# A written order for four engines, carried from the first batch to the start of the third, in a fused attention and mixture kernel

## The chip, the cores and the metric

The program runs on one core of one Trainium2 chip. The metric is device time in microseconds (us), as the median of several executions; of the kernel before there are three, 648.04, 649.50 and 650.23 us. A further execution was profiled, and all rows shown here come from that one.

## The reference

Three stages follow each other, all in float32. B = 8 batches, H = 8 heads, 576 positions, head width 64, m = 32 landmarks:

```
q_lm, k_lm = means of q, k over 18 positions each
A, Bm, C = softmax(q k_lm'), softmax(q_lm k_lm'), softmax(q_lm k')
Z = Bm' / (norm_1 * norm_inf);  six times: Z = 2 Z - Z Bm Z
x = A Z C v                          # laid out as 4608 tokens x 512
h = silu(x w_gate) * (x w_val);  x = h w_out      # 1536 hidden units
logits = x phi                       # 32 slots, softmax over tokens and over slots
out = c @ (relu((d' x) w1) w2)       # 8 experts
```

The inputs w_gate, w_val and w_out arrive as 64-bit floats and are turned into 32-bit ones on the chip.

## The kernel before, in words

A prelude computes the attention factors of batch 0 (`first_attention`, lines 424 to 594) out to two small factors: the softmax A as tiles EH and EL (a high and a low part), and WB, a product of Z, C and v. Then come eight batches, numbered 0 to 7, each of 12 units of 128 hidden units (`unit`, line 1020). A unit has two halves of 288 tokens; each half has a gate product `pg` and a value product `pv`, six matmuls each on line 1017 (`mm3`), a Silu or Tanh on ScalarE into `u`, and a multiplication on VectorE into `hT` (line 1046). Beside the units run, spread over slots between them: `g` (line 820, WB times the gate weights, cast on ScalarE to GH and subtracted on VectorE to GL), `l` (line 866, logits from `hT`), a transposition of `hT` (line 871), the attention factors of the next batch (`attention` and `a_softmax`), and the slot softmax of the batch before (`softmoe`, matmuls `m_d` on line 985). In batch 0 the conversion of the weights runs too: for each 1 MB block of the gate and value weights (`load_w`) and each 512 KB block of w_out (`load_o`) a Prelu on ScalarE (line 235) takes the upper words, and two VectorE operations (lines 251 and 252) put in the lower bits; a converted block of w_out goes to `wo_dram` (line 306) and through three small products (`m_wt`, `m_p`, `m_ps`) into P_sb, which `l` reads.

What sets the order: each engine runs its instructions in program order. A scheduler chooses that order from its own costs, unless it is told. `ORDER` (line 55) tells it: for each engine a list of positions in the traced order of that engine's instructions, `a+n` being n positions from a on. `written_order` (line 123) chains the listed instructions. What is not listed comes behind the last listed one: on TensorE in traced order, on the other engines as the scheduler has it. All transfers are issued from the sync engine (SP) one after the other; one that has to wait for its buffer holds up those behind it.

Positions that the text names. TensorE before: 0 to 14 are the fifteen 1x1 warm matmuls of line 1092, 15 to 22 the first eight score matmuls, 23 to 30 the next eight; with three warm matmuls fewer, every later position is smaller by 3. ScalarE: 1 and 2 the first two Exp, 33 the Prelu on the first block of w_out, 192 the Exp on the first half of batch 2's A, 209, 212 and 215 Silu of batch 1, 210 and 211 the casts to EH of batch 2, 237 the Silu of the first half of batch 1's last unit. VectorE: 10 the scaling that the first Exp waits for, 12 the first transposition of A, 61 a shift for the first block of w_out. GpSimd: 21 and 22 the subtractions to EL of batch 2, 23 a small addition. SP: 27 and 28 the load of v for batch 1, whose 128 KB tail is 28 and whose 1 MB main part is 27; 31, 34 and 40 blocks 5, 6 and 7 of the gate and value weights; 58 to 61 the loads of k for batch 2.

The `l` of a unit needs both halves of its `hT`; it is issued in the slots of the next unit (line 1188), and TensorE waits there if VectorE is late with `hT`.

Of the kernel before, what the change touches and what calls it, by code (L numbers as in the profile page):

```python
# [53 lines left out]

ORDER = {
    'PE': '''
# [7 lines left out]
      839+4 855+6 895+6 919+8 907+6''',  # L64
    'DVE': '''
# [8 lines left out]
      242 237 241 239 238 244 255 247 256 252+2 246 248 245 257 267+2 254 261 258 270 249''',  # L74
    'Activation': '''
# [5 lines left out]
      162 167 166 168+2 171 170 173 172 174+2 177 180 179 181 176 178 183''',  # L81
    'Pool': '''
      0 3 2 4 1 16 6 5 8 7 9+3 15 12 14 13 18''',
    'SP': '''
      0+4 7 5+2 4 14 8+2 25 17 15 18 16 23 10 22 11 21 19 24 26 12+2 29 20 28 30+2 33 32 34 40 36 35 58 37
      39 38 41+3 46 45 59 44 48 47 27 60 50+2 61 49 52 64 53+2 57 56 65+7 55 72+2 62''',
}


# [1 line left out]
def nystrom_softmoe_kernel(  # L91
# [996 lines left out]
                next(gens[c], None)  # L1088

    m = psp.tile([128, 512], F32, tag="l", name="warm")  # L1090
    for _ in range(15):
        pe.matmul(m[0:1, 0:1], one, one, start=True, stop=True)
    first_attention(side)
    in_order("silu", warm, one, AF.Silu)
# [329 lines left out]
```

## Time and profile before

| | us |
|---|---|
| median of three executions | 649.50 (648.04 to 650.23) |
| the profiled execution | 649.76 |
| its span on the core | 648.0 |
| prelude, until the first unit | 38.0 |
| batch 0 | 76.0 |
| batch 1 | 68.0 |
| batch 2, batch 3 | 65.2, 65.1 |

The batches are bounded by the first `pg` matmul of each (at 38.0, 114.0, 182.0, 247.2 and 312.3 us of the trace). Times in the views are us from the start of the span; PE is TensorE, DVE VectorE, ACT ScalarE, POOL GpSimd, SP the sync engine. What lies around the span is 1.76 us.

### The profile page before, as it was taken

The numbers are of one execution on the slowest core, as the hardware profiler recorded it, in microseconds if no ns is written. First come the engines' busy times: TensorE is split into PE (matmuls) and PEld (weight loads), VectorE is DVE, ScalarE is ACT, GpSimd is POOL, SyncE is SP. The second block draws the span as 40 slices with busy tenths as digits, with TensorE's granted clock in tenths as the row PEclk, the third lists the DMA queues.
The fourth block names the chain that finished last, engine by engine and source line by source line (L and its number), as shares of the span: only waits on it lengthen the run. The fifth ranks groups of instructions, "written<-read, shape, count | busy, mean of one in ns | idle before, by whom it ended". The sixth has DMA issues, their size and how long they took to land. (4 is left out here: it accounts for less than half of the span.)

```text
span 648.0 us, 18273 instructions
## 1 busy us (share of the span) xinstructions
PE 617.2 (95%) x7589; PEld 465.6 (72%) x7589; DVE 465.4 (72%) x1139; ACT 301.2 (46%) x761; POOL 73.0 (11%) x81
## 2 busy tenths in 40 slices
PE   6999999999999999999999999999999999999991
PEld 2866778777878787878787878787878777743560
DVE  4999989797678687868786878687856656550441
ACT  1888975383266226622662256225623532411441
POOL 0320003030013001300130013001300000010100
PEclk9999999999999999999999999999999999999996
DMA  9999871424032023302420242022310696599999
GB/s 336 389 319 330 324 250 56 143 81 129 23 127 90 8 88 129 90 4 84 135 91 3 83 138 90 3 76 72 92 58 1 218 368 233 190 327 347 348 371 331
DMA packets 63298, 106.47 MB, mean 164 GB/s; under 512 B 4976, under 2 KB 33008, under 8 KB 61680
## 3 DMA queue, kind: packets, MB, share of 16 engines
q1 hardware_dynamic: 63216, 105.32, 48.4%
q8 instruction: 59, 0.97, 0.6%
q14 instruction: 23, 0.19, 0.1%
HBM read 91.24 MB, written 12.58 MB: 160 GB/s over the span
## 5 line engine op out<-in xcount | busy, mean ns | idle before, releaser
L375 ACT ACTIVATE u<-pg 128x288 f32<-128x288 f32 x169 | 69.6, 413 | 155.3 <-PE pg L1017 151.2
L1046 DVE TENSOR_TENSOR hT<-u,pv 128x288 f32<-128x288 f32 x169 | 75.4, 448 | 36.3 <-PE pv L1017 31.1
L1017 PE MATMUL pg<-EH,GH 128*128 128x288 f32 x384 | 93.1, 323 | 0.0
L851 DVE TENSOR_TENSOR GL<-g,GH 128x512 fp32r<-128x512 f32 (+1 forms) x114 | 65.1, 598 | 35.1 <-ACT GH L837 35.1
L1017 PE MATMUL pg<-EH,GL 128*128 128x288 f32 x384 | 84.5, 297 | 0.5
L1017 PE MATMUL pv<-EH,GH 128*128 128x288 f32 x384 | 83.8, 299 | 0.0
L1017 PE MATMUL pv<-EL,GH 128*128 128x288 f32 x384 | 82.1, 295 | 0.0
L1017 PE MATMUL pg<-EL,GH 128*128 128x288 f32 x384 | 82.1, 295 | 0.0
L1017 PE MATMUL pv<-EH,GL 128*128 128x288 f32 x384 | 81.9, 294 | 0.0
L837 ACT CAST GH<-g 128x512 fp32r<-128x512 f32 (+1 forms) x114 | 54.0, 521 | 50.8 <-PE g L820 50.7
L1017 PEld LDWEIGHTS pg<-EH,GH 128*128 128x128 f32 x384 | 59.4, 189 | 24.8 <-issue 20.2
L871 DVE STREAM_TRANSPOSE HB<-hT 128x576 f32<-128x576 f32 x96 | 74.1, 773 | 1.6
L1017 PEld LDWEIGHTS pg<-EH,GL 128*128 128x128 f32 x384 | 62.0, 188 | 2.6 <-DVE GL L851 2.6
L1017 PEld LDWEIGHTS pv<-EH,GH 128*128 128x128 f32 x384 | 61.2, 188 | 2.9 <-issue 1.9
L1017 PEld LDWEIGHTS pv<-EH,GL 128*128 128x128 f32 x384 | 61.6, 188 | 0.0
L1017 PEld LDWEIGHTS pg<-EL,GH 128*128 128x128 f32 x384 | 61.5, 188 | 0.0
L1017 PEld LDWEIGHTS pv<-EL,GH 128*128 128x128 f32 x384 | 61.5, 188 | 0.0
L820 PE MATMUL g<-w,WB 64*32 64x512 f32 (+1 forms) x912 | 55.3, 534 | 0.4 <-ACT HB L329 0.3
L866 PE MATMUL l<-hT,P_sb 128*32 128x160 f32 (+1 forms) x768 | 44.7, 298 | 2.6 <-DVE hT L1046 2.2
L866 PEld LDWEIGHTS l<-hT,P_sb 128*32 128x32 f32 x768 | 15.1, 108 | 40.2 <-DVE hT L1046 15.6
L985 PE MATMUL m_d<-HB,HB 32*32 32x384 f32 x864 | 35.3, 491 | 0.0
L985 PE MATMUL m_d<-HB,DN 32*32 32x384 f32 x288 | 35.1, 491 | 0.0
(255 smaller groups left out, 939.1 us busy)
## 6 DMA issues: line engine op xcount, KB each, us to landing
k<-in_kT_dram SPq DMA_DIRECT2D x52, 288.0 KB, 3.9
ffn<-in_w_dram SPq DMA_DIRECT2D x13, 1024.0 KB, 8.6
ffn<-in_w_dram SPq DMA_DIRECT2D x24, 512.0 KB, 8.9
HB<-in_w_cat_dram SPq DMA_DIRECT2D x8, 1024.0 KB, 8.5
v<-in_v_dram SPq DMA_DIRECT2D x8, 1024.0 KB, 6.8
q<-in_qT_dram SPq DMA_DIRECT2D x28, 288.0 KB, 3.0
HB<-in_w_out_dram SPq DMA_DIRECT2D x12, 512.0 KB, 6.4
wr<-in_w_cat_dram SPq DMA_DIRECT2D x4, 1024.0 KB, 7.5
```

The lines of the kernel that those rows point to most:

```text
L375: i = act.activation(*a, **kw)
L820: pe.matmul(gs[r][32 * hp:32 * hp + 32, 0:256 * n].rearrange("p (u f) -> p u f", u=n), WB[b % 2][64 * r:64 * r + 64, hp, :], w[64 * r:64 * ...
L837: act.copy(H_, g)
L851: dve.tensor_tensor(out=GL, in0=g, in1=GH, op=ALU.subtract)
L866: pe.matmul(L[32 * c:32 * c + 32, 0:32 * k], P_sb[:, j, :], main[:, 0:k, c, :], start=j == 0, stop=j == NJ - 1)
L871: dve.transpose(HB[b % 2][:, S * j:S * j + S].rearrange("p (t r) -> p t r", r=32), hT[:, 0:S].rearrange("p (t r) -> p t r", r=32))
L985: pe.matmul(ms[a][32 * g:32 * g + 32, 0:384].rearrange("p (j f) -> p j f", j=NJ), d_of(a, g, k), hb[32 * a:32 * a + 32, :, 4 * k + g, :], ...
L1017: pe.matmul(ps[:, 0:HALF], G_t[b, j, q, sel_][h], e[:, q, ts_], start=n == 0, stop=n == 5)
L1046: i = dve.tensor_tensor(out=o, in0=u, in1=pv[:, 0:HALF], op=ALU.mult)
```

## The change

The order lists are replaced. Those of TensorE, VectorE, ScalarE and GpSimd now reach further: on TensorE 1389 positions instead of 911, out to the score matmuls in the first unit of batch 2 (185 us of the trace of before, against 130 us); on VectorE 362 instead of 261, on ScalarE 243 instead of 183, on GpSimd 25 instead of 18. They also differ from the start on, within the stretch that was already written. The list of SP becomes shorter, 36 positions instead of 73; the transfers behind it come in the scheduler's order. Three of the fifteen warm matmuls are gone, and the other twelve stand behind the first eight scores. No operation is otherwise added or removed.

```diff
--- before.py
+++ after.py
@@ -54,36 +54,49 @@
 
 ORDER = {
     'PE': '''
-      0+47 55+4 47+8 59+14 76+4 73+3 80+11 92 94+4 93 118 91 119+5 98+20 144+2 124+20 146+4 154+2 150+4
-      156+14 182+12 170+12 194+45 243+10 259 253+6 260+18 239+4 300+6 284+8 296+4 278+6 292+4 312+19 337+8
-      349+4 306+6 331+6 345+4 365 353+6 366+12 402+4 378+8 359+6 386+6 406+6 418 392+6 423+6 419+4 412+6
-      435+8 447+4 429+6 451+6 463 398+4 457+6 443+4 464+18 492+4 482+6 496+8 510+45 556+6 555 568+8 504+6
-      562+6 488+4 584+2 580+4 592+7 586+6 599+6 576+4 605+12 621+6 633+6 627+6 617+4 639+5 658+8 644+2
-      670+4 646+12 688 674+8 689+4 682+6 693+2 666+4 695+12 711+4 721+7 715+6 740+6 728+4 768+6 732+2
-      750+12 734+6 707+4 774 746+4 762+6 775+12 791+22 787+4 831+8 819+6 813+6 825+6 843+12 861+6 871+24
-      839+4 855+6 895+6 919+8 907+6''',
+      12+8 0+12 20+24 52+4 44+8 56+15 73+4 71 77 72 78+6 89 84+4 90 115 91+4 116 95+20 141+2 88 117+24
+      143+4 151+2 147+4 153+14 179+8 167+6 187+10 173+6 197+39 240+4 250+11 244+6 261+8 236+4 269+6 281+8
+      297+6 293+4 275+6 309+19 303+6 350+6 334+8 328+6 346+4 356+6 289+4 362+5 342+4 367+8 383+6 375+8
+      399+4 395+4 389+6 415 403+6 416+4 432+8 420+6 409+6 444+4 426+6 448+6 460+5 440+4 454+6 465+4 473+6
+      469+4 495+6 489+6 479+6 507+45 485+4 553+6 552 501+6 565+8 581+2 559+6 583+6 577+4 589+6 600+2 595+5
+      573+4 602+12 630+6 618+6 636 614+4 637+4 624+6 655+8 641+8 667+4 649+6 671+8 663+4 679+25 718+6
+      712+6 737+6 708+4 765+6 724+7 704+4 747+12 743+4 731+6 759+6 772+6 771 778+10 804+6 788+16 816+6
+      810+6 828+8 822+6 840+24 892+6 868+24 836+4 904+6 916+8 898+6 864+4 928+6 910+6 940+6 934+6 924+4
+      966+6 956+10 946+6 990+8 978+6 972+6 952+4 984+6 1049+6 1002+40 1061+6 1043+6 1042 1055+6 998+4
+      1071+2 1145+6 1076 1073 1080 1077 1074 1078 1075 1084 1079 1081+2 1088 1085 1083 1087 1091 1095 1092
+      1096 1089 1093 1086 1090 1094 1097 1099+2 1104 1101 1098 1102+2 1107 1111 1115 1106 1110 1119 1105
+      1123 1114 1118 1109 1108 1122 1112 1126 1130 1134 1113 1116+2 1121 1120 1138 1125 1129 1133 1124
+      1127 1137 1142 1141 1128 1132 1136 1140 1131 1135 1139 1144 1143 1151+14 1171+8 1183+2 1067+4 1179+4
+      1165+6 1185+12 1241+8 1197+14 1215+2 1223+6 1217+6 1211+4 1229+6 1253+2 1235+6 1255+12 1249+4 1283+2
+      1267+16 1285+16 1307+6 1301+6 1313+6 1329+14 1319+6 1343+6 1355+6 1365+8 1349+6 1373+8 1325+4 1361+4
+      1381+8''',
     'DVE': '''
-      1 0 3 2 6 4 7 5 12 24 9 8 10 23 14+4 21 61 18 22 20 27 19 25 11 13 26 42 32 34 33 35+2 43 37 48 41
-      38 44 62 45+3 52 49 57 54 53 50 39 102 29 28 31 68 40 58 30 56 97 59+2 51 65 55 63+2 75 69 73 71 74
-      66 72 70 77 98 79 76 67 78 80+2 99 103 85+2 84 91 83 82 88 87 89+2 93+2 92 100+2 106 109 127 136 96
-      120 105 108 95 113 104 107 119 114 129 117 111 116 118 139 112 121 115 110 131 123 135 125 128 138
-      126 133+2 137 130 122 223 132 146 142 147 150 124 140 153 145 157 167 149 151 143+2 154 164 152 172
-      156 160+3 148 158 141 155 163 159 168 166 169+2 165 175 171 185 181 189 182+3 186 179 190+3 188
-      193+2 180 197 201 187 204 198 203 199 176 202 195 205+2 209 207 215 196 173 212+2 210 177 214 216
-      174 229 219 211 217 220 178 221 218 224 222 227+2 200 208 226 231 225 232+2 230 236 235 234 240 243
-      242 237 241 239 238 244 255 247 256 252+2 246 248 245 257 267+2 254 261 258 270 249''',
+      1 0 3 2 6 4 7 5 12 61 24 8+3 14+4 22+2 21 18 20 27 19 25 11 13 26 42+2 32+6 45 41 57 28 46 44 47 38
+      49 62 53 48 29 58 50 39 97 40 31 56 52 54 51 102 59+2 65 30 68 55 63+2 69 73 66 75 70+2 74 72 79 77
+      103 67 76 80 78 81 84 91 85+2 82+2 88 99 98 90 89 93 92 94 101 100 87 105 108 106 109 127 120 95 129
+      104 116 136 113 96 114 118 111+2 115 117 135 107 122 138 119 121 130+2 123 125 132+2 110 124 126 128
+      146 137 134 150 140 147 145 139 141 143 149 154 144 157 153 148 142 151 167 164 160 152 163 161+2
+      159 155 166 172 158 175 165 168 170 169 171 181 183 182 184 223 185+2 156 191 188 179 192 187 189
+      194 193 173 201 190 197 204 198 180 199 196 195 205+2 203 202 207 176 215 212+2 177 174 209 214 216
+      210 217 211 219+3 218 222 224 178 225 228 200 226 208 229 227 232+2 230 234+2 239 231 244 238 242
+      245 243 241 236+2 247 240 255+2 252 257 248 253+2 258 246 250 267 259 251 272 260 273 262 261 268
+      270 264 263 265 269 271 249 282 266 280 275+2 274 316 286 325 287+2 292 290 289 294 303 283 297 304
+      328 293 298 305 291 284 299 333 285 301 300 302 308 306 310 277 309 278 334 279 311 295 313+2 317
+      315 312 307 352 322+2 326 324 320 327 321 329+3 336 332 337+3 335 347 340 346 343+2 349 345 348
+      341+2 350 353 296 355 351 359 356 354 358 362 357 364+2 361 366''',
     'Activation': '''
-      2 1 3 33 6 4 7 15 59 10 8 13 9 11+2 17 14 16 5 21 20 57 25 38 18+2 24 27 23 29+2 26 42 28 31 22 34+3
-      40 39 51 41 37 44 43 45 47 63 53 48+3 55 46 54 52 75 56 66 83 60+3 58 64 67 65 68+2 71 78 72 74 73
-      79 70 77 80 93 76 87 85 81+2 84 0 86 90 92 88 91 111 96 98 97 99 106 100 94 112 107 105 95 108 89
-      109+2 113 103 114+2 101+2 117+2 104 119 123 116 131 120+2 124 127 122 126 128 125 129+2 138 133+2
-      132 135+3 141 140 142 139 143 32 146+3 144+2 149 151 154 152 155+4 160 159 161 153 150 164 163 165
-      162 167 166 168+2 171 170 173 172 174+2 177 180 179 181 176 178 183''',
+      33 1+3 6+2 4+2 8 10 12 9 11 15 14 17 13 16 59 21 57 20 25 18+2 38 24 27 29+2 23 26 42 28 31 22 34+3
+      39+3 51 37 44 43 47 45 53 46 49 48 50 83 55 54 56 66 52 63 58 61 60 65 62 67+2 64 69 77 75 71+2 70
+      76 73+2 78+2 93 87 80+2 85 84 82 90 111 86 91 96 92 97 100 98 112 88 106 99 95 89 94 107+2 110 109
+      101 113 102 0 114+2 103 105 118 104 119 116+2 127 123 120+3 128 124 129 125 130 126 138 133 131 136
+      134+2 132 32 137 141+3 139+2 146 144+2 152 149 148 147 151 156 154+2 158 157 150 159+3 163 153 164+2
+      162 166+2 169+2 168 171+6 181 177 180 179 183 178 184 182 187 189 191 185 194 188 190 186 199+3 195
+      193 197 196 202 198 205 203 206 204 209 207+2 212 192 213+4 218 217 220+2 210 222 224 223 219 225+4
+      231 229+2 232+2 235 234 236+2 211 238+3 248 243''',
     'Pool': '''
-      0 3 2 4 1 16 6 5 8 7 9+3 15 12 14 13 18''',
+      1 0 3 2 4 6 5 8 7 10 9 11+2 15 13+2 16+3 26 20 19 23 21+2''',
     'SP': '''
-      0+4 7 5+2 4 14 8+2 25 17 15 18 16 23 10 22 11 21 19 24 26 12+2 29 20 28 30+2 33 32 34 40 36 35 58 37
-      39 38 41+3 46 45 59 44 48 47 27 60 50+2 61 49 52 64 53+2 57 56 65+7 55 72+2 62''',
+      0+4 7 5+2 4 14 8 25 15 17 9+2 16 21 18 23 11+2 20 22 26 13 24 29 19 30 33 40 32 31 35+2 34''',
 }
 
 
@@ -1088,7 +1101,7 @@
                 next(gens[c], None)
 
     m = psp.tile([128, 512], F32, tag="l", name="warm")
-    for _ in range(15):
+    for _ in range(12):
         pe.matmul(m[0:1, 0:1], one, one, start=True, stop=True)
     first_attention(side)
     in_order("silu", warm, one, AF.Silu)
```

## Rows read from the trace of the kernel before

**Rows 1.** The page: busy time, share of the span and instructions by engine.
```profile
PE 617.2 (95%) x7589; PEld 465.6 (72%) x7589; DVE 465.4 (72%) x1139; ACT 301.2 (46%) x761; POOL 73.0 (11%) x81
```

**Rows 2.** Windows, by stage: stretch, its length, busy us by engine, PE clock, DMA share, GB/s.
```profile
0.00:38.00 38.00, 29.94 (x351) 20.11 (x351) 28.42 (x71) 19.67 (x45) 9.60 (x14) 1.00 0.98 360
38.00:114.00 76.00, 75.14 (x848) 57.98 (x845) 72.70 (x165) 58.16 (x135) 8.89 (x7) 1.00 0.70 247
114.00:182.00 68.00, 66.23 (x858) 51.79 (x857) 53.27 (x132) 31.16 (x81) 10.59 (x10) 1.00 0.33 102
182.00:247.20 65.20, 65.02 (x827) 51.13 (x826) 51.21 (x127) 29.35 (x77) 8.28 (x8) 1.00 0.25 78
```

**Rows 3.** Waits of TensorE, 15.5 to 185 us: total us, times, longest us.
```profile
PE l L866 <- DVE hT L1046: 1.6, 2, 0.9
PE m_v L724 <- DMA v<-in_v_dram: 0.7, 1, 0.7
...
PE m_c L606 <- ACT CE L449: 0.5, 1, 0.5
...
PE m_n L743 <- DVE RV L759: 0.2, 1, 0.2
```

**Rows 4.** Timeline of TensorE in the prelude: start, us, operation, [idle before].
```profile
0.87 0.88 PE L1092 MATMUL warm<-one 1*1 1x1 f32 x30 [0.87 <-POOL one L1058]
...
10.12 0.70 PE L606 MATMUL m_a<-qk,ks 64*32 64x288 f32 x4 [0.18 <-DVE qs L396]
...
16.54 4.18 PE L879 MATMUL warm<-cst 128*128 128x160 f32 x24
```

**Rows 5.** Timeline of VectorE in the prelude.
```profile
13.36 0.17 DVE L496 TENSOR_SCALAR stat<-stat 128x2 f32<-128x2 f32 x1
...
16.58 0.42 DVE L251 TENSOR_SCALAR HB<-HB 128x512 int32<-128x512 int32 x1
```

**Rows 6.** Timeline of ScalarE in the prelude.
```profile
13.61 1.28 ACT L372 ACT_TABLE_LOAD   x1 [13.61 <-DVE stat L496]
14.90 0.29 ACT L372 ACTIVATE nrm<-m_a,stat 128x32 f32<-128x32 f32 x1
...
15.72 0.69 ACT L235 ACTIVATE HB<-HB 128x512 f32<-128x512 f32 x1
```

**Rows 7.** Timeline of SP: transfers that it issues.
```profile
31.21 0.49 SPq L225 DMA_DIRECT2D v<-in_v_dram  x1
...
70.12 0.42 SPq L224 DMA_DIRECT2D v<-in_v_dram  x1
```

**Rows 8.** Waits of SP up to 130 us: total us, times, longest us.
```profile
SPq L306 <- DVE HB L252: 8.6, 2, 4.8
```

**Rows 9.** Waits of ScalarE for transfers, 38 to 92 us.
```profile
ACT HB L235 <- DMA HB<-in_w_out_dram: 0.9, 1, 0.9
...
ACT w L235 <- DMA wr<-in_w_cat_dram: 0.6, 1, 0.6
```

**Rows 10.** The page: `m_d`, over all eight batches: busy us, mean ns, idle before.
```profile
L985 PE MATMUL m_d<-HB,HB 32*32 32x384 f32 x864 | 35.3, 491 | 0.0
```

**Rows 11.** Timeline of ScalarE in batch 1: cast to EH, and a late Silu.
```profile
143.59 0.68 ACT L797 CAST EH<-AT 128x576 fp32r<-128x576 f32 x1 [0.28 <-DVE AT L789]
...
178.21 0.41 ACT L375 ACTIVATE u<-pg 128x288 f32<-128x288 f32 x1 [1.18 <-PE pg L1017]
```

**Rows 12.** Timeline of GpSimd: both subtractions to EL of batch 2.
```profile
143.38 2.82 POOL L798 TENSOR_TENSOR EL<-AT,EH 128x576 fp32r<-128x576 f32 x2 [2.11 <-ACT EH L797]
```

**Rows 13.** Timeline of TensorE about the end of batch 1.
```profile
178.01 0.42 PE L1017 MATMUL pv<-EH,GH 128*128 128x288 f32 x2
178.27 0.43 PE L1017 MATMUL pv<-EL,GH 128*128 128x288 f32 x2
...
178.89 0.47 PE L866 MATMUL l<-hT,P_sb 128*32 128x160 f32 x8
...
182.01 0.42 PE L1017 MATMUL pg<-EH,GH 128*128 128x288 f32 x2
```

## The prediction

> **What bounds the kernel now.** I read the page first: TensorE is busy for 617.2 of 648.0 us, 95% of the span, VectorE for 72% [rows 1]. So what the change can save is idle time of TensorE, 31 us in all, and only the part of it that lies before 185 us, where the new lists end. The windows by stage say where that is [rows 2]. In the prelude TensorE is idle for 8.1 us (38.00 - 29.94). In batch 0 it is idle for 0.9 us (76.00 - 75.14), with VectorE idle for only 3.3 us (76.00 - 72.70): two engines are nearly full there and order can give little. Batch 1 takes 68.0 us, with TensorE idle for 1.8 us, while batch 2, of the same shape, takes 65.2 us, with 0.2 us idle. So the order there is already tight, and batch 1 is 2.8 us above it. The list of waits of TensorE then names the gaps one by one [rows 3]. From batch 2 on a microsecond gained stays gained: the window of batch 2 shows no idle time in which it could be lost, and the batches behind it run the same order.
>
> I make the sum against the profiled execution's own 649.76 us (span 648.0 and 1.76 around it). That is 0.26 us above the median of the runs, 649.50; I don't correct for it, since one run in three lies on either side.
>
> **The prelude.** The first work of ScalarE before is the Exp of the small softmax. A table load of 1.28 us stands just ahead of it; it starts 0.08 us after the scaling on VectorE (13.36 + 0.17 = 13.53, load at 13.61), so all of it lies on the path: the Exp runs at 14.90 [rows 5, 6]. In the new list position 33, a Prelu, comes first on ScalarE. Before, that Prelu ran at 15.72 with the table that the Exp had loaded [rows 6], so one table serves both, and the load now stands ahead of the Prelu, which waits for the first block of w_out and for nothing else. Ahead of the block come eight loads of 295 KB; with its own 524 KB these are 2.9 MB, 8 us at the 360 GB/s of the prelude [rows 2], and with some 3 us for the start (an estimate) it lands by 11 to 11.5 us. Then load and Prelu end by 11.5 + 1.28 + 0.69 = 13.5 us, and the Exp starts as soon as its scaling is done. Against that, VectorE has the shift (position 61) ahead of the scaling now, 0.42 us with some overlap, say 0.35 [rows 5]: the Exp starts at 13.53 + 0.35 + 0.1 = 14.0 instead of 14.9, which is 0.9 us earlier. The second cost is the warm matmuls. Fifteen took 0.88 us [rows 4], twelve take 0.70. They stood at 0.87 us, where TensorE had nothing to do; now they stand between the first eight scores and the next eight, which before waited 0.18 us for VectorE at 10.12 us [rows 4]. So up to 0.5 us of them is not covered. I take 0.2, since part of it is caught by the waits of VectorE that follow. What comes next on TensorE are score matmuls that wait 0.5 us for a copy on ScalarE behind those Exps [rows 3], then 4.18 us of larger warm matmuls up to 20.7 us [rows 4], then the chain of the iteration. The warm ones are queued, so all of it moves by what the copy moves: -0.7 us. Bounds: -1.3 (the whole load) and +0.5 (block late, warm matmuls in the way).
>
> **Batch 0.** Work of VectorE and TensorE is only permuted, so the gain is bounded by TensorE's idle time, 0.9 us. Most of that is one wait: `m_v` for the load of v of batch 1, 0.7 us [rows 3]. The tail of that load was issued at 31.21 us, so the buffer was free then, but the main part stood far back in SP's list and went out at 70.12 [rows 7]. In the new list neither part is named; they head what the scheduler may place, so I expect them right behind the list's end. That takes the wait away. The price is that 1.05 MB, at the 360 GB/s that the prelude shows [rows 2] 2.9 us of transfer, comes ahead of weights. Some of these have no room: ScalarE waited 0.9 us for a block of w_out and 0.6 us for a block of the other weights [rows 9]. Against that, block 7 (position 40) is now ahead of 5 and 6, and not behind the one that waits. ScalarE has room (58.16 of 76.00 us busy [rows 2]), so a late Prelu reaches TensorE only where the products of w_out stand in its order. I take -0.7 for the wait and +0.2 for late weights, together -0.5. Bounds: -0.9 and +2.9, the whole transfer.
>
> **Batch 1.** On TensorE this batch was in traced order for the most part. Two `l` wait 1.6 us for `hT`, and one product of the iteration 0.2 us [rows 3]. In the new list the `l` that waited first stands behind three half products more than before, the second between the matmuls of `m_d`. A half product is three pairs of matmuls that start 0.26 us apart [rows 13], so 0.8 us: `hT` gets 2.4 us where it lacked 0.9 at most. The gain is 1.8 us. Bounds: 0, if the waits only change their place, and -2.8, down to the length of batch 2.
>
> ScalarE gets one more pair of table loads here: the Exp on A of batch 2 (192) now stands between the Silus 212 and 215, and an Exp of the first run is followed by Silus as before. By the row a load is 1.28 us, with the Exp 0.01 us behind it [rows 6], so the pair costs ScalarE 2.6 us. It falls where TensorE runs `m_d`, which asks nothing of ScalarE and takes 35.3 / 8 = 4.4 us in each batch [rows 10]. I cost it at nothing, with +1.3 as the other end: one load in front of a Silu that TensorE waits for.
>
> The Trainium skill (ScalarE: Activation LUTs, What ACT_TABLE_LOAD costs) puts 1.38 us of drain on top of the load, 2.66 us for a switch. By that rule the pair would be 5.3 us, 0.9 more than `m_d` covers, and the sum 647.9 instead of 647.0. The row speaks against it: nothing but the load lies between the scaling and the Exp, so I give this 0.02, inside the first rival.
>
> **The end of batch 1.** The A of batch 2 is made late now: its second cast to EH (211) comes behind the Silu 237, and EL behind that on GpSimd. The steps are Silu 0.41, cast 0.68 [rows 11] and one subtraction of 1.4 (2.82 for two [rows 12]), with three handovers of some 0.1: 2.8 us. They start when the `pg` of the last unit's first half ends. Before, TensorE had 4.0 us of work from there to batch 2 (178.01 to 182.01 [rows 13]), of which one `l` of 0.5 now comes later: 3.5 us. The cover is 0.7 us. I put 0.2 us on it, the smallest wait that a row of this stretch shows [rows 3]; the ends are 0 and 1.4, EL late by its own length. If TensorE runs faster there, the cover shrinks by the same.
>
> **The sum.** 649.76 - 0.7 - 0.5 - 1.8 + 0.2 = 646.96, so 647.0 us, 0.4% below the median of before. Its own range is 645.5 to 648.2.
>
> **Rivals.** What a measurement of this kernel can tell from no change is 0.3%, 1.95 us: faster is below 647.55, slower above 651.45.
>
> First, the waits move. The `hT` that an `l` waited for is late because VectorE is; in the new list VectorE has other work ahead of it, and the wait appears at the next `l` or at a `pg` whose buffer isn't free. For it: VectorE is busy for 53.27 of 68.0 us in batch 1, and batch 0 has no room at all [rows 2]. Against it: batch 2 has the same load and 0.2 us idle. Then half of the batch 1 and prelude terms is left: 649.76 - 0.35 - 0.9 - 0.2 = 648.3 us.
>
> Second, slower: SP blocks. A transfer that the scheduler thinks ready stands ahead of a weight block and waits for its buffer; before, two writes of converted w_out waited 8.6 us in SP, one of them 4.8 [rows 8]. If one more of that length stands ahead of a block with no room [rows 9], the Prelu, VectorE's two operations and the products of w_out that TensorE has in its fixed order are late by about 4.8 us. It decides from the point where the block lands later than the 1 us or so that ScalarE can make up. 649.76 - 0.7 - 1.8 + 0.2 + 4.8 = 652.3 us. Against it: batch 2 runs in the scheduler's order of transfers with next to no wait, though with a DMA share of 0.25 where batch 0 has 0.70 [rows 2].
>
> Third, everything closes: the prelude by the whole load, batch 0 by its idle time, batch 1 to the length of batch 2: 649.76 - 1.3 - 0.9 - 2.8 = 644.8 us.
>
> **Chances.** Forecast 0.45, of which four fifths lie below 647.55 (0.36) and the rest within 0.3%; waits move 0.24, all within; SP blocks 0.16, all slower; everything closes 0.15, all faster. That makes faster 0.51, same 0.33, slower 0.16. The range runs from 644.0, a little below the third rival, to 651.5, at the edge of the second, whose upper part is what it leaves out.
>
> **What would show it.** In the profile of the changed kernel: the first table load of ScalarE before 13 us and the iteration's first product before 20.2 us; batch 0 between 75.0 and 76.0 us long and no wait of `m_v` for v; the waits of `l` gone and batch 1 at 66 to 66.5 us; no wait of a batch 2 `pg` or `pv` for EL above 0.3 us. Wrong would be a prelude that ends at 38 us or later, waits of `m_p` or `g` behind late Prelus in batch 0, or new waits for `u`, `hT` or EL in batch 1 as long as the old ones.

## The result: 1.1% slower, and all of it in batch 0

The changed kernel takes 656.72 us (median of four executions, 654.89 to 657.46); the kernel before, beside it on the same chip, 649.12 us. The ratio is 1.0111, with a 95% interval of 1.0094 to 1.0128. The prediction was 647.0, range 644.0 to 651.5: wrong in sign, and outside its range. What happened lies nearest to the second rival, at 1.7 times its price (8.2 us for 4.8).

Windows by stage, cut at the first `pg` of each batch as in [rows 2] (batch 2 begins with a `pv` in the new order, and is cut there; its first `pg` is at 189.62), with the same columns:

```profile
0.00:36.70 36.70, 28.29 (x336) 19.48 (x336) 27.63 (x71) 19.54 (x44) 9.38 (x13) 1.00 0.96 361
36.70:120.90 84.20, 78.17 (x857) 59.04 (x851) 69.92 (x164) 57.91 (x134) 8.51 (x8) 0.96 0.68 236
120.90:188.00 67.10, 67.10 (x852) 52.24 (x851) 53.42 (x130) 33.81 (x84) 8.29 (x8) 1.00 0.31 94
188.00:253.80 65.80, 65.63 (x833) 51.26 (x833) 52.18 (x131) 29.26 (x77) 10.57 (x10) 1.00 0.24 77
```

Against [rows 2] the prelude is 1.3 us shorter, batch 0 8.2 longer (84.20 - 76.00), batch 1 0.9 shorter, batch 2 0.6 longer. Batches 3 to 6 are unchanged, and the stretch from batch 7 on is 1.2 longer (143.1 against 141.9). Together that is +7.8; the spans differ by 7.7 (655.7 - 648.0). Within batch 0, TensorE's idle time grew from 0.9 to 6.0 us and its busy time by 3.0, from 75.14 to 78.17, with a clock of 0.96: one part is waiting, most of the other the same work at a lower clock. TensorE's waits in batch 0 (us in total, times, longest):

```profile
PE m_p L350 <- ACT CE L659: 5.1, 1, 5.1
PE pg L1030 <- ACT u L388: 0.6, 1, 0.6
```

The waits of [rows 3] for `hT` and for v are gone, as forecast, and one wait of 5.1 us is new. Line numbers are 13 higher than before. `m_p` needs a buffer that ScalarE's copy to CE (line 659) frees. ScalarE's timeline at that point (start, us, operation, idle time before and what ended it) shows why the copy is late:

```profile
55.50 0.41 ACT L659 COPY CE<-m_c 128x288 f32<-128x288 f32 x1
63.04 0.66 ACT L248 ACTIVATE HB<-HB 128x512 f32<-128x512 f32 x1 [7.13 <-DMA HB<-in_w_out_dram]
63.60 1.12 ACT L248 ACTIVATE w<-HB 128x1024 f32<-128x1024 f32 x1
64.63 0.38 ACT L659 COPY CE<-m_c 128x288 f32<-128x288 f32 x1
```

The first of two copies runs at 55.50. Ahead of the second the new list has the Prelu on block 5 of w_out, and ScalarE stands still for 7.13 us until that block lands. TensorE has work until 59.9 us:

```profile
59.49 0.44 PE L1030 MATMUL pv<-EH,GL 128*128 128x288 f32 x2
65.06 0.66 PE L350 MATMUL m_p<-HB 128*32 128x128 f32 x8 [5.13 <-ACT CE L659]
...
66.77 0.68 PE L1030 MATMUL pv<-EH,GL 128*128 128x288 f32 x2
...
73.74 0.43 PE L1030 MATMUL pv<-EL,GH 128*128 128x288 f32 x2
```

The same pair of matmuls takes 0.68 us behind the stop and 0.43 or 0.44 ahead of it and later. The windows give the clock (the number before the DMA share):

```profile
56.00:60.00 4.00, 3.93 (x37) 2.68 (x35) 2.25 (x6) 0.00 (x0) 0.00 (x0) 1.00 1.02 349
60.00:64.00 4.00, 0.00 (x0) 0.00 (x0) 0.27 (x1) 0.96 (x2) 0.00 (x0) 1.00 1.04 426
64.00:68.00 4.00, 2.94 (x22) 1.86 (x22) 3.22 (x6) 3.82 (x8) 0.00 (x0) 0.62 0.71 280
68.00:72.00 4.00, 4.00 (x37) 2.21 (x34) 3.25 (x7) 2.28 (x4) 0.00 (x0) 0.53 0.64 200
72.00:76.00 4.00, 4.00 (x63) 3.39 (x69) 2.63 (x6) 2.68 (x7) 0.00 (x0) 1.00 0.57 168
```

From 65.06 to about 71.8 us TensorE runs at half clock (1.2 GHz, not 2.4). The windows of 0.62 and 0.53 lose 0.38 and 0.47 of 4 us each, 3.4 us together. With the wait of 5.1 that makes 8.5 us, a little more than the 8.2 of batch 0; the rest of the batch is slightly shorter than before.

Why is the block late? SP's issues (in order: w_out blocks 2 and 3 in one row; block 7 of the gate and value weights, called weight block 7 from here; weight block 5; w_out block 4; weight block 6; both parts of v of batch 1; weight block 8; w_out block 5):

```profile
30.24 7.50 SPq L286 DMA_DIRECT2D HB<-in_w_out_dram  x2
37.80 1.19 SPq L275 DMA_DIRECT2D wr<-in_w_cat_dram  x1
...
39.64 0.33 SPq L275 DMA_DIRECT2D wr<-in_w_cat_dram  x1
...
45.06 0.37 SPq L286 DMA_DIRECT2D HB<-in_w_out_dram  x1
45.47 0.48 SPq L275 DMA_DIRECT2D HB<-in_w_cat_dram  x1
46.00 0.43 SPq L237 DMA_DIRECT2D v<-in_v_dram  x1
46.48 0.65 SPq L238 DMA_DIRECT2D v<-in_v_dram  x1
47.77 0.33 SPq L275 DMA_DIRECT2D HB<-in_w_cat_dram  x1
...
51.14 0.39 SPq L286 DMA_DIRECT2D HB<-in_w_out_dram  x1
```

w_out block 5 goes out at 51.14, at once when its staging buffer is free, and lands at 63.02. Ahead of it in a full queue are weight block 6 (first read 9.1 us after it lands), v (first read 29 us after) and weight block 8 (7.7 us after). For the two weight blocks that is less room than it looks: ScalarE's stop of 7.13 us lies within the 9.1 of block 6 and puts off the read of block 8. And the 7.50 us of the first row are w_out block 3, waiting for its buffer; weight blocks 7 and 5 stand behind it although their own buffers are free earlier (in a run below they go out at 34.4 and 34.8 us). The view of SP's waits has that one with its releaser:

```profile
SPq L286 <- DVE HB L265: 6.8, 1, 6.8
```

### The profile page after: what moved, and what is told of

It is laid out like the page before. It is cut to its first block, busy times and chain, and to the rows that moved or that the text cites. A ratio compares the mean times of both kernels' runs of the same rounds, so it can differ in the third digit from the quotient of the medians.

```text
span 655.7 us, 18278 instructions
## 1 busy us (share of the span) xinstructions
PE 620.0 (95%) x7583; PEld 466.6 (71%) x7583; DVE 462.8 (71%) x1139; ACT 303.6 (46%) x763; POOL 72.5 (11%) x81
## 5 line engine op out<-in xcount | busy, mean ns | idle before, releaser
L879 PEld LDWEIGHTS l<-hT,P_sb 128*32 128x32 f32 x768 | 15.5, 108 | 37.2 <-DVE hT L1059 11.7
```

What stands on the lines that cost most here:

```text
L879: pe.matmul(L[32 * c:32 * c + 32, 0:32 * k], P_sb[:, j, :], main[:, 0:k, c, :], start=j == 0, stop=j == NJ - 1)
```

## The experiments

All are compared with the kernel before on the same chip; batch lengths are from each one's profiled execution. "New" and "old" lists are those of the changed kernel and of the kernel before. Line numbers shift by one or so with the length of the lists.

**Which half does it: engines or transfers?** Three runs pair the halves anew. First the new lists of the four engines with SP's old list:

```diff
 'SP' in the changed kernel:
-      ... 30 33 40 32 31 35+2 34
+      ... 28 30+2 33 32 34 40 36 35 58 37 39 38 41+3 46 45 59 44 48 47 27 60 50+2 ... 55 72+2 62
```

> The new lists of TensorE, VectorE, ScalarE and GpSimd, with SP's list of before (73 positions). Theory 1, the transfers' order makes the loss (the 5.1 us wait in batch 0 and the half clock behind it, 8.2 us together): batch 0 back to 76 us or less, 648 us or faster, with 1.3 us of the prelude and 0.9 of batch 1 kept. Rival, ScalarE's new list asks for the sixth block of w_out too early for any order of transfers: the wait on that block stays above 3 us and the time at 653 us or more.

663.41 us, ratio 1.0216 (1.0190 to 1.0241), batch 0 87.1 us, and the prelude ends at 40.0 us, not 36.7. That is slower still, so "the old transfers cure it" falls. Here weight block 7 goes out only at 45.19, and ScalarE waits in other places.

Second, the changed kernel's 36 positions of SP and then the old order of what is left:

```diff
 'SP' in the changed kernel:
-      ... 30 33 40 32 31 35+2 34
+      ... 30 33 40 32 31 35+2 34 28 58 37 39 38 41+3 46 45 59 44 48 47 27 60 50+2 ... 55 72+2 62
```

> The changed kernel, with SP's 37 unlisted transfers put back behind the 36 listed ones in the sequence that they had before. Theory 1a, it is the scheduler's order behind the list (v of batch 1 ahead of the weights) that makes the loss: the sixth block of w_out lands at 59 to 60 us instead of 63.0, the wait of TensorE is under 2 us, 649 to 652 us. Theory 1b, it is the listed 36 (SP held for 6.8 us by the fourth block of w_out at 30 us, the two big blocks behind it): 654 us or more.

658.68 us, 1.0157 (1.0124 to 1.0190), batch 0 85.8 us: the scheduler's order of the remainder was not the worse one.

Third, the old engine lists with the new list of SP (the edit of the first run, the other way round):

```diff
 'SP' in the kernel before:
-      ... 28 30+2 33 32 34 40 36 35 58 37 39 38 41+3 46 45 59 44 48 47 27 60 50+2 ... 55 72+2 62
+      ... 30 33 40 32 31 35+2 34
```

> The kernel before, with only SP's list changed to the new 36 positions and the scheduler's order behind them. Theory 1: slower than before by 3 to 8 us, with waits of ScalarE for weight blocks in batch 0 that add up to more than 5 us. Rival (ScalarE's new list): no loss beyond 1 us.

667.88 us, 1.0288 (1.0268 to 1.0307), batch 0 88.1 us: a loss of 18.7 us, more than twice the 3 to 8 expected, of which 4.9 lie in the prelude (it ends at 42.9 us). Each set of engine lists runs badly with transfers that were not made for it. In the changed kernel the queue is full (DMA share near 1.0 from 44 to 64 us), so each block's place should decide. In the next runs the new engine lists stay and single places of SP's list are moved.

**v of batch 1 last.** The scheduler's order of the remainder written out, with v (27, 28) at its end:

```diff
-      ... 30 33 40 32 31 35+2 34
+      ... 30 33 40 32 31 35+2 34 37+3 41+3 58+2 44+2 60+2 46+3 27+2
```

> The changed kernel, with SP's transfers behind the list in the sequence that the scheduler gave them, but for v of batch 1 (1.2 MB), which comes 15 transfers later. By theory 1a taken at its narrowest (this one load) 3.3 us of transfer leave the way of the sixth block of w_out: it lands at 59.7 us, TensorE waits 1.8 us instead of 5.1 and the clock may hold, 650 to 653 us. By theory 1b or the rival on ScalarE's list the time stays within 1 us of 656.7.

654.05 us, 1.0073 (1.0057 to 1.0088), a little above the range given. w_out block 5 lands at 60.24, 2.8 us earlier, which is v's 1.05 MB, and batch 0 is 81.1 us. So v ahead of the block costs 3.1 us in the profile. TensorE's waits, and two windows behind the first of them:

```profile
PE m_p L351 <- ACT CE L660: 2.2, 1, 2.2
PE pg L1031 <- ACT u L389: 1.0, 1, 1.0
PE m_v L738 <- DMA v<-in_v_dram: 0.8, 1, 0.8
```

```profile
60.00:64.00 4.00, 1.81 (x16) 1.26 (x14) 2.21 (x4) 3.68 (x9) 0.00 (x0) 0.90 0.90 354
64.00:68.00 4.00, 4.00 (x43) 2.31 (x43) 4.00 (x9) 3.50 (x6) 0.00 (x0) 0.68 0.51 161
```

The wait for v of [rows 3] is back, 0.8 us for 0.7. And the clock is halved for a while behind a stop of 2.2 us. Length alone does not decide that: behind a stop of 2.6 us in the run with SP's old list (TensorE idle from 51.1 to 53.7 us) and one of 2.3 us in the second run (61.0 to 63.3 us) the granted clock stays at 1.00.

**w_out block 5 first.** Besides v, weight blocks 6 (34) and 8 (37) go behind it (39):

```diff
-      ... 30 33 40 32 31 35+2 34
+      ... 30 33 40 32 31 35+2 38+2 34 37 41+3 58+2 44+2 60+2 46+3 27+2
```

> The changed kernel's lists, but with w_out block 5 issued as soon as its staging buffer is free, ahead of weight blocks 6 and 8 (in the changed kernel these went out 5.7 and 3.4 us before it and were needed only 9.1 and 7.7 us after they landed), and v of batch 1 last. Theory 1 (the loss of batch 0 is one block behind transfers that had room): block 5 lands at 53 to 54 us instead of 63.0, the waits of ScalarE for it (7.1) and of TensorE for m_p (5.1) go, the clock stays at full in 60 to 72 us, batch 0 is 76 to 77.5 us long instead of 84.2, and the time 648.5 to 650.5 us. Rival (the new lists of the engines are slower in batch 0 by themselves; another block is late next, 6 or 8): a wait of 3 us or more for a weight block takes its place, batch 0 stays at 79 us or more, time 652 to 655.

651.31 us, 1.0044 (1.0018 to 1.0069), above the range given, batch 0 78.3 us, and the block lands at 55.24. The 53 to 54 expected was too early; weight blocks 7 and 5, still late in the queue, are the likely reason. Another 2.8 us are gone, and the rival has a part: ScalarE now waits 3.3 us for weight block 6.

```profile
PE pg L1031 <- ACT u L389: 1.4, 1, 1.4
PE m_p L351 <- ACT CE L660: 1.3, 1, 1.3
```

```profile
60.00:64.00 4.00, 2.73 (x30) 1.78 (x28) 2.07 (x4) 3.99 (x8) 0.00 (x0) 1.00 1.03 425
64.00:68.00 4.00, 3.78 (x69) 2.55 (x69) 4.00 (x9) 3.75 (x9) 0.00 (x0) 1.00 0.99 359
```

Behind both stops of this run the clock stays at full.

**Nothing behind the block that waits for its buffer.** Weight blocks 5 (31) and 7 (40) ahead of w_out block 3 (33) as well. A second place differs from the last run: weight block 6 (34), which ScalarE waited for there, is ahead of w_out block 5 again, while weight block 8 and v stay behind it:

```diff
-      ... 30 33 40 32 31 35+2 34
+      ... 30 31 40 33 32 35+2 34 38+2 37 41+3 58+2 44+2 60+2 46+3 27+2
```

> As the run with block 5 first, and weight blocks 5 and 7 also go out ahead of w_out block 3, whose buffer is free only at 37.4 us (the changed kernel held both behind it and its DMA share fell to 0.53 at 36 to 40 us); block 6 stays ahead of w_out block 5. Theory 1: the waits of ScalarE for the two blocks (1.2 and 0.6 us) go as well, and what TensorE waited for behind them (0.6 for u and a part of the m_a waits of 6.4): batch 0 75.5 to 76.5 us, time 647.5 to 649.5, no slower than the kernel before. Rival (those waits were covered by room on ScalarE): as the other run, within 0.3 us of it.

647.89 us, 0.9989 (0.9974 to 1.0004): the whole loss is undone by SP's order alone. Batch 0 is 74.7 us, shorter than before. Stages of this run, and TensorE's one large wait from batch 0 to the end of batch 1:

```profile
36.60:111.30 74.70, 74.39 (x858) 57.42 (x852) 69.59 (x164) 57.88 (x134) 8.51 (x8) 1.00 0.74 263
111.30:180.30 69.00, 67.86 (x852) 52.20 (x851) 53.39 (x129) 33.78 (x84) 8.27 (x8) 1.00 0.31 92
180.30:246.40 66.10, 65.91 (x834) 51.39 (x834) 52.25 (x131) 29.24 (x77) 10.58 (x10) 1.00 0.25 77
```

```profile
PE m_d L999 <- issue: 1.1, 1, 1.1
```

Batch 1, though, is 69.0 and not 67.1: TensorE stops in the middle of the products `m_d`, with no releaser that the profile shows.

**The hold alone.** Only the places of weight blocks 5 and 7; the rest stays with the scheduler, v and weight blocks 6 and 8 ahead of w_out block 5 with it:

```diff
-      ... 30 33 40 32 31 35+2 34
+      ... 30 31 40 33 32 35+2 34
```

> The changed kernel with one edit in its list of transfers: weight blocks 5 and 7 ahead of w_out block 3, so that they don't wait with it for a buffer; everything behind the list stays with the scheduler, v of batch 1 ahead of w_out block 5 with it. Theory (three terms that add: the held blocks, v, and blocks 6 and 8 ahead of block 5, as the steps of 3.1, 2.8 and 3.7 us between the runs say): some 2.5 us of the transfers' idle time at 36 to 44 us are used, block 5 lands at 60 to 61 instead of 63.0, TensorE's wait at m_p is 2 to 3 us and the clock still falls behind it; batch 0 79.5 to 81.5, time 652 to 654.5. Rival (the hold is the root, the rest is late because of it): block 5 lands by 56, batch 0 below 77, time 648 to 649.5. Other rival (only v and blocks 6 and 8 matter): block 5 at 62.5 or later, time 656 to 657.

655.28 us, 1.0100 (1.0083 to 1.0117), above the range given, and by the times alone not to be told from the changed kernel. The block lands at 60.85 and batch 0 is 81.1 us, as the theory had it. Those 3.1 us come from one profiled execution of each kernel, the changed kernel's the slowest of its four and this one's the fastest; the medians differ by 1.4 us. The transfers' share at 36 to 40 us is 1.00, against 0.53 in the changed kernel. TensorE waits 4.2, not 2 to 3, since it comes to `m_p` earlier:

```profile
PE m_p L350 <- ACT CE L659: 4.2, 1, 4.2
```

```profile
36.00:40.00 4.00, 3.88 (x42) 2.85 (x41) 4.00 (x9) 2.27 (x6) 0.58 (x1) 1.00 1.00 417
...
60.00:64.00 4.00, 1.09 (x10) 0.71 (x11) 1.66 (x4) 3.13 (x7) 0.00 (x0) 0.64 1.01 421
64.00:68.00 4.00, 4.00 (x28) 2.51 (x26) 3.86 (x8) 3.07 (x6) 0.00 (x0) 0.50 0.54 189
```

**The engines' order, with the transfers left late.** ScalarE's Prelus 77 and 75 behind five instructions that don't need the block, and VectorE's shift 116 likewise:

```diff
 'Activation':
-      ... 69 77 75 71+2 70 76 73+2 78+2 ...
+      ... 69 71+2 70 76 73+2 77 75 78+2 ...
 'DVE':
-      ... 104 116 136 113 96 114 118 111+2 115 ...
+      ... 104 136 113 96 114 111+2 116 118 115 ...
```

> The changed kernel with the transfers as they are; only ScalarE's Prelu of w_out block 5 and the next one stand behind five instructions that don't need the block (copies to CE and GH, two Silus, one copy), and VectorE's shift of the block behind six. If the price of the late block is a matter of what stands behind it in the engines' order, TensorE's wait of 5.1 us at m_p falls to 2 to 3 us, at m_wt of block 5 now, the clock falls for less long, batch 0 is 79 to 81.5 us and the time 651.5 to 654. If the order is all of it, 648 to 650; if only the transfers count, the block is as late for TensorE as before and the time stays at 656 to 657.

655.16 us, 1.0105 (1.0079 to 1.0132), batch 0 81.8 us, both a little above the ranges given. In the profile 2.4 us of the 8.2 come back; the median is 1.6 us below the changed kernel's, which the intervals don't tell apart. TensorE's waits:

```profile
PE m_c L619 <- ACT P_sb L357: 3.0, 1, 3.0
PE pg L1030 <- ACT u L388: 1.3, 1, 1.3
```

By the profile the late block is the root, and what stands behind it in the engines' order adds to the loss; by the times alone the second half is not shown.

**The table load alone.** The kernel before, with ScalarE's position 33 moved to the front:

```diff
 'Activation' in the kernel before:
-      2 1 3 33 6 4 7 15 ...
+      33 2 1 3 6 4 7 15 ...
```

> The kernel before with one instruction moved: ScalarE's Prelu of w_out block 0 first, so that the table load stands ahead of the Exps. If the prelude's gain of the changed kernel (1.3 us, 36.7 against 38.0) is the table load, the first Exp comes 0.9 to 1.2 us earlier, batch 0 starts at 36.7 to 37.2, and as batch 0 is full the time is 0.8 to 1.3 us below the kernel before, 647.9 to 648.4. Rival (the gain came from VectorE's and TensorE's new order of the prelude): start at 37.7 or later, time 648.8 to 649.5.

648.63 us, 0.9990 (0.9978 to 1.0003), which the measurement does not tell from no change. In its profile batch 0 starts at 36.7 us and the first Exp at 13.43, against 38.0 and 14.90 [rows 6].

**Lists cut in batch 1, and the stop in `m_d`.** Two runs with the transfers of the run that undid the loss. In the first the engine lists end where the old ones did, TensorE's with position 923 and the others at the same time:

```diff
 'PE':
-      ... 868+24 836+4 904+6 916+8 898+6 864+4 928+6 ... 1361+4 1381+8
+      ... 868+24 836+4 904+6 916+8
```

> The transfers of the run with both corrections, and the new lists of the engines cut where the kernel before's ended (15 us into batch 1), so that batch 1 stands in traced order again. Theory: the longer lists are worth 0.3 us in batches 1 and 2 together (133.2 us before, 132.9 in the changed kernel), because what the waits of l give, 1.8 us, is paid back as longer matmuls of pv and m_d; and the stop of TensorE in the products m_d (1.1 us with no releaser, 2.0 us longer in all) is not in the traced order. So the l waits of some 1.6 us are back, batches 1 and 2 take 133 to 133.5 us together (135.1 in the run with both), and the time is 646.0 to 646.8. Rival (my prediction's reading, the l waits are worth their whole length): batches 1 and 2 at 134.5 or more, time 647.5 to 648.5.

647.81 us, 0.9985 (0.9975 to 0.9995), median above the range given. Batches 1 and 2 take 133.1 us (68.0 and 65.1), as the theory said, and the stop is gone.

In the second there are 15 small warm matmuls, not 12:

```diff
-    for _ in range(12):
+    for _ in range(15):
         pe.matmul(m[0:1, 0:1], one, one, start=True, stop=True)
```

> The run with both corrections of the transfers, with 15 small warm matmuls as the kernel before had, not 12: TensorE's instructions behind them are the same, each three places later in its stream. If the stop in m_d comes from where the stream is fed to the engine (a packet of the instruction queue falls in 149 to 150 us, in the stop's place, and in the changed kernel in 154 to 155, 1.5 us ahead of m_d), it moves or goes: batch 1 67 to 67.5 us, time 645.7 to 646.5. Rival (it comes from the transfers of that stage, whatever the stream): the stop of 1.0 to 1.4 us stays at the same products, batch 1 at 69, time 647.6 to 648.3.

647.45 us, 0.9983 (0.9974 to 0.9992), median above the range given. This run and the one before it are faster than the kernel before, clear of the noise but by 0.2% only, and by the ratios 1.3% faster than the changed kernel; the measurement does not tell the two apart. The stop is gone; the stages:

```profile
0.00:36.70 36.70, 28.45 (x342) 19.57 (x342) 27.65 (x71) 19.51 (x44) 9.39 (x13) 1.00 0.98 367
36.70:111.50 74.80, 74.39 (x858) 57.42 (x852) 69.64 (x164) 57.88 (x134) 8.51 (x8) 1.00 0.74 262
111.50:178.60 67.10, 67.10 (x853) 52.25 (x851) 53.39 (x129) 33.78 (x84) 8.28 (x8) 1.00 0.31 94
178.60:244.30 65.70, 65.51 (x833) 51.13 (x833) 52.18 (x131) 29.23 (x77) 10.58 (x10) 1.00 0.26 77
```

Its span is 2.5 us below that of before, its median 1.3 (648.71 for the kernel before in that comparison): the later part of the program scatters by as much (see the tail below).

## Why the prediction was wrong

**Batch 0: -0.5 forecast, +8.2 measured.** This is the step that failed, in two sentences of it. The first is "+0.2 for late weights". I saw that v would head what the scheduler places, and priced its whole transfer at 2.9 us as a bound; the run with v last measured 3.1. But I took a value near the other end, on the ground of two small waits [rows 9]. I did not follow the list of 36 positions through SP: block 3 of w_out waits there for a buffer (6.8 us) with two weight blocks behind it, worth 3.1 us in the profile of the run with that alone. Nor did I ask what the scheduler would put ahead of w_out block 5 besides v: weight blocks 6 and 8, worth 2.8 us more once v was away. With the hold gone and v and block 8 behind w_out block 5 (block 6 ahead of it again) batch 0 is 9.5 us shorter.

The second is "ScalarE has room, so a late Prelu reaches TensorE only where the products of w_out stand in its order". Room is an average. ScalarE runs in order, and behind the late Prelu stands a copy that frees a buffer for TensorE. That copy, not a product of the block, is what TensorE waited for. Among my signs of being wrong I had named waits of `m_p` behind late Prelus, but I gave them no term.

And I had no term for the clock: behind a stop of 5.1 us came some 6.7 us at half clock, 3.4 us on top. The bound of +2.9 was exceeded because it held neither the held blocks nor this.

The second rival named the mechanism, an SP that waits for a buffer with weights behind it, at 4.8 us. Its place differs in part: the buffer was that of a load in the written list, not of a write that the scheduler placed, and more than half of the loss lay in order without any wait of SP.

The bound for a gain in batch 0, TensorE's idle 0.9 us, did not hold either. With the transfers mended the batch is 1.3 and 1.2 us shorter than before (74.7 and 74.8 for 76.0), since its busy time falls too, from 75.14 to 74.39: permuted work did not keep its length.

**The prelude: -0.7 forecast, -1.3 measured**, the end that I had as a bound. With the Prelu moved alone the prelude is the same 36.7 us, so the table load accounts for all of it, as far as single profiles tell (with the new lists the prelude ends at 36.4 to 37.3 us, but for the run with SP's old list). The new lists' shift and warm matmuls delay the first Exp (14.13 against 13.43 in that run), as I had it, but nothing of that is left at the end of the prelude.

**Batch 1: -1.8 forecast; batches 1 and 2 together gained 0.3** (132.9 against 133.2). The waits for `hT` did go, and TensorE is busy for all of the 67.10 us. But one `l` of batch 1, eight matmuls, moved behind the start of batch 2 (`l` counts 88 for 96 in batch 1 and 104 for 96 in batch 2); its 0.4 us explain most of batch 2's +0.6. And busy time grew. The same groups in batch 1, before and after (count, busy us, mean ns, idle):

```profile
L1017 PE MATMUL pv<-EH,GH 128*128 128x288 f32 x48 | 10.4, 297 | 0.0
...
L985 PE MATMUL m_d<-HB,DN 32*32 32x384 f32 x36 | 4.3, 491 | 0.0
```

```profile
L1030 PE MATMUL pv<-EH,GH 128*128 128x288 f32 x48 | 11.3, 317 | 0.0
...
L998 PE MATMUL m_d<-HB,DN 32*32 32x384 f32 x36 | 4.6, 491 | 0.0
```

`pv` took 0.9 us more, and `m_d`, with its second group that went from 4.3 to 4.7, 0.7 more: 1.6 of the 1.8. Where a matmul follows another kind, the first one takes longer (0.51 to 0.54 us for a pair, against 0.42 to 0.43 behind its own kind), and the new order has more such changes. The traced order, with 0.9 us of its `l` waits left, came within 0.2 us of it. That more changes of kind cause it is read from the rows, not tried by itself.

**The end of batch 1: +0.2 forecast, no wait of a batch 2 product seen.** EL was finished at 187.00 us, 1.0 ahead of batch 2. The extra pair of table loads in batch 1 is there and costs TensorE nothing, as costed. The Trainium skill (ScalarE: Activation LUTs, What ACT_TABLE_LOAD costs) puts 1.38 us of drain on top of each load, by which the pair would have outlasted its cover. The trace does not agree: on ScalarE the Exp starts 0.01 us behind its load (155.00 + 1.28, Exp at 156.29), and TensorE has no idle time in batch 1.

**The tail**, 1.2 us longer in the changed kernel, has the same instructions and the same waits of TensorE. It was 141.9 to 143.1 us in the profiles of these kernels, and its second half runs with a DMA share of 1.0 to 1.1. I take it for scatter of the transfers; that was not tried.

What held is the direction of the gain, and about half of its size: with SP's order mended, the new lists give 647.9 us, and 647.5 with 15 warm matmuls. That is 1.2 us (not clear of the noise) and 1.3 us below the kernel before in the same comparisons, where 2.5 were forecast (649.50 - 647.0), and that it comes near is in part luck, since the terms are others. In the profile of the best one the prelude gives -1.3, batch 0 -1.2, batches 1 and 2 -0.4 and the tail +0.4.

## What to carry to other kernels

A written order of engines and the order of its transfers are one object: in a stretch where the DMA queues are full, follow each block from its issue through the queue to the in-order instruction that first reads it, and to what stands behind that instruction. An engine's mean load says nothing on that. A list of transfers should have nothing ready behind an entry that waits for a buffer, and what is first read tens of microseconds later goes last.

## What the runs showed of the hardware

TensorE's granted clock went to half for some microseconds behind stops of 5.1, 4.2, 3.0 and 2.2 us, and stayed at full behind stops of 1.3 and 1.4, but also behind the stops of 2.6 and 2.3 us in the first two runs. So a stop can cost more than its length: 8.5 us for 5.1, and behind the one of 2.2 us the windows of 0.90 and 0.68 lose 1.7 us (0.10 and 0.32 of 4 us each).

TensorE can stop with no releaser in the trace. In three runs (SP's old list, w_out block 5 first, and the one that undid the loss) `m_d` of batch 1 stood still for 1.0 to 1.4 us (some 2 us in all), and with three more small matmuls at the start of the stream, over 130 us earlier, the last of the three runs had no such stop. Without them it stopped at 150.70 to 151.84 us, and a packet of the instruction queue came at 149 to 150, within `m_d`; with them the packet came at 142 to 144, and `m_d` began at 146.85. The transfers of that stage were the same in the pair. Five other runs with the same stream as the three (the changed kernel is one) did not stop: there the packet came 1.6 to 3.1 us ahead of `m_d` and 7.0 to 8.7 us behind the packet before it, while in the three it came 2.5 to 2.7 us into `m_d` and 12.8 to 13.0 us behind. In the run with the lists cut, whose stream is another, a packet came 0.6 us into `m_d` without a stop. That the stream was fed too late fits all of these; it is the likely cause, and was not tried apart.
